# Order of the early loads in an attention and mixer kernel: q and k of pair 2 ahead of the sink rows

## The chip, the cores and the metric

The kernel runs on one core of a Trainium2 chip. A core has four compute engines that appear below by short names: TensorE (PE, with its weight loads as PEld), VectorE (DVE), ScalarE (ACT) and GpSimd (POOL). A fifth one, SyncE (SP), computes nothing and issues data transfers (DMAs); POOL issues some too. The transfers of both are carried out by the same 16 DMA engines. Every engine works through its own list of instructions in order and waits for others through semaphores.

The metric is the device time of one execution in microseconds (us). Less is better.

## The reference

The inputs are q, k and v (batch 4, 8 heads, 768 positions, head dimension 64) and four weight matrices. First comes attention in which each position sees a window of 128 positions up to itself and, beside it, the first 4 positions, the sinks:

```python
keep = is_sink | in_window            # pos < 4, or 0 <= query - key < 128
scores = np.where(keep, q @ k.T / sqrt(64), -1e9)
a = softmax(scores)
x = (a @ v) with the heads side by side    # (4, 768, 512)
```

Its result goes through a mixer of two stages with a residual each:

```python
h = np.maximum(x.T @ w_tok1, 0) @ w_tok2   # over the 768 positions, through 256
u = x + h.T
h2 = np.maximum(u @ w_ch1, 0) @ w_ch2      # over the 512 channels, through 1536
out = u + h2                               # (4, 768, 512) float32
```

## The kernel before

**Pairs.** Attention is done two heads at a time. There are 16 pairs, four for each batch; pair 0 to 3 are those of batch 0. For a pair, q and k are brought to bfloat16, turned on PE so that the head dimension lies on the partitions, multiplied, put through the exponential on ACT, masked, and multiplied with v. The two mixer stages of a batch follow and are interleaved with the attention of the next one.

**Early loads.** SP loads q and k of pairs 0 to 3 as float32 straight into the tile `early`: `load_raw` (L121) issues one DMA for q and one for k, 384 KB each. They are cast on the core, by ACT and DVE for pairs 0 to 2 and by POOL for pair 3 (`cast`, L1303; `copy`, L169). All other loads of inputs and weights are issued by POOL, which has them cast to bfloat16 on the way (`load_cast`, `load_v`, `load_w`).

**Sink rows.** The first four rows of v of each head are needed as a separate matrix, in which two pairs share a group of 32 partitions. The float32 tile `v_sink_f` (L238) is cleared by DVE; then four small DMAs on SP (L240 to L247, 2 KB each) put the sink rows of batch 0 into it, each followed by a DVE instruction that sets its column of ones. One POOL instruction (queued at L1310, run through `copy`, L173) casts it to `v_sink`. PE multiplies with `v_sink` in every half of every pair's last product (`pv`).

**What sets the order.** `in_order` keeps the instructions of an engine in the order in which the program issues them. The first part of the program is issued by hand: loads of pairs 0 and 1 (L186), a few matmuls on ones, masks and constants, the sink rows (L240), the loads of pairs 2 and 3 (L248), and v of pair 0 on POOL (L249). What follows is ordered by a planner (`Plan`) which simulates the engines with costs written into the program, takes whichever step could begin first and so fixes each engine's list. When the early loads land it doesn't work out: they stand as constants, for the casts at L1307 and for the sinks at L1310. On POOL its list begins with v of pair 0 and q of pair 4 and goes on with the cast of the sinks, v of pairs 1 and 2, `w_tok1`, v of pair 3, the cast of q of pair 3, `w_tok2`, the cast of k of pair 3, and more weights.

The lines of the planner that give the landing times:

```python
for p, at in enumerate(((3900.0, 5300.0), (7500.0, 8600.0), (11300.0, 12500.0), (13500.0, 14700.0))):
    for n, name in enumerate(("q_bf", "k_bf")):
        queue((name, p), cast(p, n, at[n]))
v_sink = Op({"POOL": 650.0}, lambda e: copy(e, v_sink0, v_sink_f), [landed(9000.0)])
```

Of the kernel before, what the change touches and what calls it, by code (L numbers as in the profile page):

```python
# [16 lines left out]
def kernel(  # L17
# [23 lines left out]
    NHP = H // 2  # L41
# [64 lines left out]
    def rows_of(pidx, n):  # L106

        b, hp = pairs[pidx]
        return (q, k)[n][b, 2 * hp:2 * hp + 2].rearrange(
            "h (j p) d -> p h j d" if pidx >= BY_DMA else "h (p j) d -> p h j d", j=NT,  # L110
        )
# [9 lines left out]
    def load_raw(pidx):  # L121
        raw = []
        for n in range(2):
            f = early[:, 2 * pidx + n]
            in_order(nc.sync.dma_start(out=f, in_=rows_of(pidx, n).rearrange("p h j d -> p h (j d)")))  # L125
            raw.append(f.rearrange("p h (j d) -> p h j d", j=NT))
        return raw
# [26 lines left out]
    def load_v(pidx):  # L154
        b, hp = pairs[pidx]
        v_aug = v_buf[pidx % NV]
        in_order(nc.gpsimd.dma_start(  # L157
            out=v_aug.rearrange("p i t d -> p (i t) d")[:, :, 0:D],
            in_=v[b].rearrange("h s d -> (h s) d")[2 * hp * S:2 * (hp + 1) * S].rearrange("(n p) d -> p n d", p=P),
        ))  # L160
        return v_aug
# [24 lines left out]
    raws = {p: load_raw(p) for p in range(2)}  # L186
# [50 lines left out]
    ODD = D // 2  # L237
    v_sink_f = singles.tile([P, NHP, 2, D1], FP32)  # L238
    in_order(nc.vector.memset(v_sink_f, 0.0))
    for n in range(4):  # L240
        i, odd = n // 2, n % 2
        rows = slice(D * i + ODD * odd, D * i + ODD * odd + n_sink)
        in_order(nc.sync.dma_start(
            out=v_sink_f[rows, odd::2, i, 0:D],
            in_=v[0].rearrange("(p o i) s d -> i o s p d", i=2, o=2)[i, odd, 0:n_sink],
        ))
        in_order(nc.vector.memset(v_sink_f[rows, odd::2, i, D:D1], 1.0))  # L247
    raws.update({p: load_raw(p) for p in range(2, NHP)})  # L248
    vs[0] = load_v(0)  # L249

    w_tok1 = singles.tile([P, NT, DTOK], BF16)
# [1141 lines left out]
```

## Time and profile before

| | |
|---|---|
| median of 3 runs | 196.14 us (195.31 to 196.88) |
| the profiled execution | 194.44 us |
| its span, first to last instruction | 192.7 us |
| PE busy in the span | 185.8 us |
| POOL busy in the span | 60.5 us, nearly all of it in the first half |
| granted clock of PE | 1.00 |

The profile is of one execution. Its times count from the start of the span. A row of the timeline gives the start, the time, the engine, the line of the kernel, the operation, what it writes and reads, and how many instructions are merged; in brackets stands how long the engine sat idle before it and what ended that. An engine named with a q (SPq, POOLq) is the part that issues DMAs. A row of the chain of work gives start, duration and what ran or was waited for. The time of a busy engine is not work alone: PE's instructions overlap, so a PE that is shown busy may still have small gaps between its instructions.

### The profile page before, as it was taken

To read this page: it belongs to the slowest core of one execution; us is meant where nothing else is said; L and a number is where in the kernel's file an instruction comes from. 1 tells how busy PE (TensorE), PEld (TensorE's weight loads), DVE (VectorE), ACT (ScalarE), POOL (GpSimd) and SP (SyncE) were. 2 spreads that over 40 slices of the span, in tenths; PEclk is the share of its full clock that TensorE was granted. 3 is DMA by queue.
4 is the path that set the end of the run, shared out by engine and by line. 5 is a ranking of instruction groups with operands and counts; after the bars stand their busy time and mean duration, and the time that the engine had idled before them with its cause. 6 is when DMAs were issued, how large, how long until landed. Compare 5 with 4: busy or idle time off the path is not lost.

```text
span 192.7 us, 5797 instructions
## 1 busy us (share of the span) xinstructions
PE 185.8 (96%) x2491; PEld 129.8 (67%) x2491; DVE 134.4 (70%) x299; ACT 106.3 (55%) x183; POOL 60.5 (31%) x78
## 2 busy tenths in 40 slices
PE   6898999999999999999999999999999999999993
PEld 1345995567764564666668888767678886567882
DVE  4768777898976647689778787847678771047672
ACT  4898767878865216879663433778642005764000
POOL 7299663765944951537810000000000000000000
PEclk9999999999999999999999999999999999999999
DMA  5999999999999999999999953400040435000016
GB/s 186 287 293 172 203 202 194 187 194 181 176 122 147 188 186 187 195 184 155 111 138 149 161 117 143 178 0 3 0 82 3 83 112 218 0 0 3 27 67 234
DMA packets 82138, 26.34 MB, mean 137 GB/s; under 512 B 69952, under 2 KB 79296, under 8 KB 82112
## 3 DMA queue, kind: packets, MB, share of 16 engines
q0 software_dynamic: 56864, 11.80, 74.8%
q1 hardware_dynamic: 25248, 14.17, 34.0%
q8 instruction: 19, 0.31, 0.7%
q14 instruction: 7, 0.06, 0.1%
HBM read 26.75 MB, written 6.29 MB: 171 GB/s over the span
## 4 chain that ended last, share of the span: by engine, by line
PE 88%; DMA 6%; DVE 1%; POOL 1%; SPq 0%; ACT 0%; issue 0%
PE ps_mx L164 77%; PE ps_sc L164 9%; DMA early<-in_q_dram 6%; PE ps_sc L496 1%; PE ps_mx L167 1%; PE ps_mx L496 1%; DVE kT L173 0%; SPq L125 0%; POOL k_bf L173 0%; POOL q_bf L173 0%; ACT qT L171 0%; POOL w_tok L182 0%; DVE o_sb L1100 0%; DVE v1T L179 0%; DVE ps_sc L545 0%
## 5 line engine op out<-in xcount | busy, mean ns | idle before, releaser
L164 PE MATMUL ps_mx<-uT,w_ch 128*128 128x384 bf16 x384 | 69.2, 326 | 0.0
L177 ACT ACTIVATE v1T<-ps_mx 128x384 bf16<-128x384 f32 x83 | 40.7, 490 | 36.1 <-PE ps_mx L164 35.5
L612 ACT ACTIVATE pT<-ps_sc 128x1024 bf16<-128x1024 f32 (+1 forms) x48 | 44.2, 954 | 19.6 <-PE ps_sc L164 19.4
L164 PEld LDWEIGHTS <-w_ch 128*128 128x128 bf16 x384 | 35.9, 98 | 21.3 <-issue 0.9
L164 PE MATMUL ps_mx<-w_ch,v1T 128*128 128x256 bf16 (+1 forms) x168 | 29.6, 318 | 0.0
L164 PEld LDWEIGHTS <-v1T 128*128 128x128 bf16 x234 | 22.5, 98 | 10.0 <-issue 0.5
L164 PEld LDWEIGHTS <-early 128*128 128x128 bf16 x222 | 21.3, 98 | 2.8
L164 PEld LDWEIGHTS <-w_tok 128*128 128x128 bf16 x240 | 19.5, 98 | 3.6 <-issue 0.2
L157 POOL DMA_DIRECT2D v_aug<-in_v_dram x16 | 16.7, 1050 | 7.5 <-PE ps_mx L164 5.1
L1255 DVE TENSOR_TENSOR early<-v1T 128x1152 bf16<-128x1152 bf16 x12 | 8.9, 754 | 13.8 <-ACT v1T L177 13.6
L829 DVE TENSOR_TENSOR u_sb<-ps_mx,x_sb 128x512 bf16<-128x512 f32 (+1 forms) x24 | 15.4, 654 | 2.9 <-PE ps_mx L164 2.6
L148 POOL DMA_DIRECT2D q_bf<-in_q_dram x16 | 13.2, 827 | 12.2 <-DMA q_bf<-in_q_dram 4.0
L164 PE MATMUL ps_mx<-w_sums,early 128*128 128x256 bf16 x126 | 15.9, 273 | 0.0
L164 PE MATMUL ps_mx<-v_aug,pT 128*128 128x65 bf16 x352 | 15.6, 193 | 0.0
L1100 DVE TENSOR_TENSOR o_sb<-ps_mx,u_sb 128x256 f32<-128x256 f32 x28 | 11.7, 422 | 5.3 <-PE ps_mx L164 5.1
L148 POOL DMA_DIRECT2D k_bf<-in_k_dram x16 | 13.3, 840 | 6.6 <-DMA v_aug<-in_v_dram 3.3
L164 PEld LDWEIGHTS <-pT 128*128 128x128 bf16 x352 | 13.8, 97 | 2.3 <-issue 0.4
L620 DVE TENSOR_TENSOR pT<-pT,mask_main 128x768 bf16<-128x768 bf16 (+1 forms) x25 | 14.6, 614 | 0.3 <-ACT pT L612 0.3
L164 PE MATMUL ps_sc<-qT,kT 64*32 64x160 bf16 (+3 forms) x480 | 14.2, 233 | 0.4 <-DVE ps_sc L545 0.2
L164 PE MATMUL ps_mx<-h1T,w_tok 128*128 128x256 bf16 (+1 forms) x120 | 14.2, 251 | 0.0
L164 PEld LDWEIGHTS <-kT 64*32 64x32 bf16 (+1 forms) x512 | 7.0, 91 | 9.1 <-issue 8.0
L164 PE MATMUL ps_mx<-x_sb,w_tok 128*128 128x256 bf16 (+1 forms) x120 | 12.2, 251 | 0.0
(84 smaller groups left out, 201.8 us busy)
## 6 DMA issues: line engine op xcount, KB each, us to landing
out_dram<-o_sb SPq DMA_DIRECT2D x22, 256.0 KB, 2.8
v_aug<-in_v_dram POOLq DMA_DIRECT2D x16, 192.0 KB, 9.4
w_ch<-in_moe_w_ch_dram POOLq DMA_DIRECT2D x8, 384.0 KB, 10.4
early<-in_q_dram SPq DMA_DIRECT2D x4, 384.0 KB, 5.2
early<-in_k_dram SPq DMA_DIRECT2D x4, 384.0 KB, 6.4
k_bf<-in_k_dram POOLq DMA_DIRECT2D x16, 96.0 KB, 11.3
q_bf<-in_q_dram POOLq DMA_DIRECT2D x16, 96.0 KB, 8.8
q_bf<-in_q_dram POOLq DMA_DIRECT2D x4, 192.0 KB, 9.4
```

The lines of the kernel that those rows point to most:

```text
L148: in_order(nc.gpsimd.dma_start(out=out[:, h], in_=rows[:, h]))
L157: in_order(nc.gpsimd.dma_start(out=v_aug.rearrange("p i t d -> p (i t) d")[:, :, 0:D], in_=v[b].rearrange("h s d -> (h s) d")[2 * hp * S:2 ...
L164: in_order(nc.tensor.matmul(*args, skip_group_check=True, **kwargs))
L167: in_order(nc.tensor.transpose(out, in_, ident))
L177: in_order(nc.scalar.activation(out, in_, AF.Relu))
L496: in_order(nc.tensor.transpose(outs[x][columns], block, ident[rows, rows]))
L612: in_order(nc.scalar.activation(part(tiles["pT", p][:, :, ds(2 * g, 2)]), of_keys(tiles["ps_s", p, g])[:, :, 0:width(g)], AF.Exp, scale=scale,
L620: in_order(nc.vector.tensor_tensor(out=pt, in0=pt, in1=m, op=ALU.mult))
L829: in_order(nc.vector.tensor_tensor(out=u_part(b, g, s0, n), in0=tiles["ps_u", b, g, s0], in1=x_sb[b][:, s0:s0 + n, c0:c0 + cn], op=ALU.add,))
L1100: in_order(nc.vector.tensor_tensor(out=o_sb, in0=ps, in1=u_rows(b, st)[:, g, cols] if first else o_sb, op=ALU.add,))
L1255: lambda e, n=n, x=x, y=y, how=how: in_order(nc.vector.tensor_tensor(out=v1_sums[:, n, ds(j, SUMMED)], in0=of(x), in1=of(y), op=how,)), deps,
```

## The change

The loads of q and k of pair 2, two DMAs on SP, are issued between the clearing of `v_sink_f` and the four small loads of the sink rows. Those of pair 3 stay behind the small loads. No instruction is added or taken away, no tile moves, and the planner's constants are the same.

```diff
     v_sink_f = singles.tile([P, NHP, 2, D1], FP32)
     in_order(nc.vector.memset(v_sink_f, 0.0))
+    raws[2] = load_raw(2)
     for n in range(4):
         i, odd = n // 2, n % 2
         rows = slice(D * i + ODD * odd, D * i + ODD * odd + n_sink)
...
         in_order(nc.vector.memset(v_sink_f[rows, odd::2, i, D:D1], 1.0))
-    raws.update({p: load_raw(p) for p in range(2, NHP)})
+    raws[3] = load_raw(3)
     vs[0] = load_v(0)
```

## The prediction

> **What bounds the kernel now.** I read the page's head first, then the chain of work that ended last.
>
> ```profile
> span 192.7 us, 5797 instructions
> PE 185.8 (96%) x2491; PEld 129.8 (67%) x2491; DVE 134.4 (70%) x299; ACT 106.3 (55%) x183; POOL 60.5 (31%) x78
> ```
>
> TensorE (PE) fills 96% of the span. So the question for any edit at the front is whether it delays PE's steady work. The chain of work shows what PE waits for there (start, duration, what):
>
> ```profile
> 1.76 5.26 DMA early<-in_q_dram
> ...
> 7.04 6.76 DMA early<-in_q_dram
> ...
> 13.86 0.82 POOL q_bf L173
> 14.68 0.65 POOL w_tok L182
> 15.33 0.84 POOL k_bf L173
> ...
> 16.22 0.35 PE ps_mx L505 x12
> ```
>
> The reader is to see a chain of loads (q of pair 1, whose landing at 7.02 us lets q of pair 3 be issued, which lands at 13.80), then a stretch on POOL, which casts q and k of pair 3 with a weight load's issue between them, and then PE. Busy time by stretches (bounds, length, then PE, PEld, DVE, ACT, POOL, PE clock, DMA share, GB/s) and PE's waits after 17 us say what a delay at this place is worth:
>
> ```profile
> 14.00:17.00 3.00, 1.92 (x69) 1.49 (x69) 2.07 (x4) 2.12 (x4) 3.00 (x5) 1.00 2.18 172
> ...
> 22.00:187.00 165.00, 164.81 (x2170) 117.84 (x2168) 117.47 (x250) 88.87 (x157) 44.30 (x52) 1.00 1.08 121
> ```
> ```profile
> PE ps_sc L164 <- DVE ps_sc L545: 0.2, 1, 0.2
> ```
>
> From 14 to 17 us PE is busy 1.92 of 3 us and POOL all of it. From 22 to 187 us PE is busy 164.81 of 165 us, and in the list of PE's waits from 17 to 188 us that one wait of 0.2 us is all there is. So almost nothing later can swallow a delay: what PE loses before 17 us, the end loses too, less about 0.2.
>
> **The change, part by part.** SP issues its twelve loads in this order (start, issue time):
>
> ```profile
> 2.26 0.47 SPq L125 DMA_DIRECT2D early<-in_k_dram  x1
> 2.81 1.36 SPq L243 DMA_DIRECT2D v_sink_f<-in_v_dram  x4
> 4.22 0.40 SPq L125 DMA_DIRECT2D early<-in_q_dram  x1
> 4.88 0.39 SPq L125 DMA_DIRECT2D early<-in_k_dram  x1
> 7.04 0.37 SPq L125 DMA_DIRECT2D early<-in_q_dram  x1
> 8.20 0.37 SPq L125 DMA_DIRECT2D early<-in_k_dram  x1
> ```
> ```profile
> SPq L125 <- DMA early<-in_q_dram: 1.8, 1, 1.8
> SPq L125 <- DMA early<-in_k_dram: 1.0, 2, 0.8
> ```
>
> These waits fit one rule: a load waits for the landing of the one eight places ahead of it. The tenth (k of pair 2, at 4.88) waits for the second, the eleventh (q of pair 3) for the third, the twelfth for the fourth. The change moves the fifth to eighth loads (sinks) behind the ninth and tenth. The eleventh and twelfth keep their places and the loads that they wait for, so the issues at 7.04 and 8.20 stay. Pair 2 is issued right behind 2.26 + 0.47, at about 2.75 and 3.25, some 1.5 us sooner. The sinks, 1.36 us of issuing, start at about 3.75; the last two of them become the ninth and tenth, and the last would be out at about 5.2, before the next load's 7.04. No instruction is added; nothing on SP ends later.
>
> What moves is the place in the queue. When do the data land? The engines that read them show it:
>
> ```profile
> 8.21 0.56 DVE L173 CAST k_bf<-early 128x768 bf16<-128x768 f32 x1 [0.60 <-DMA early<-in_k_dram]
> ...
> 11.69 0.57 DVE L173 CAST k_bf<-early 128x768 bf16<-128x768 f32 x1 [1.46 <-DMA early<-in_k_dram]
> ```
> ```profile
> 9.10 0.61 POOL L173 CAST v_sink<-v_sink_f 128x520 bf16<-128x520 f32 x1 [3.51 <-DMA v_sink_f<-in_v_dram]
> 9.66 2.21 POOL L157 DMA_DIRECT2D v_aug<-in_v_dram  x2
> 11.86 0.84 POOL L182 DMA_DIRECT2D w_tok<-in_moe_w_tok_dram  x1
> 12.67 1.04 POOL L157 DMA_DIRECT2D v_aug<-in_v_dram  x1
> ```
>
> k of pair 1 starts its cast at 8.21, the sinks theirs at 9.10, k of pair 2 at 11.69, each ending a wait for its load. The sinks were all issued by 4.17 (2.81 + 1.36), yet their 8 KB (32 rows of 64 floats) are read only 0.89 us behind k of pair 1, issued in front of them. I read this as a first-in, first-out queue: a small load waits for the large ones ahead. Put behind k of pair 2, the sinks should be ready at 11.69 + 0.89 = 12.58, **3.48 us later**. (That k of pair 2 lands sooner I cost at nothing: the stream ahead of it is the same but for 8 KB; the other end is the first rival.)
>
> The Trainium skill, page "DMA: Bandwidth & Descriptors", section "Queues, rings and completion order", states that each DMA engine takes a ring's descriptors in order, but that a load may use fewer than all 16 engines and completion between loads is then not in order. By this rule a sink could land ahead of the slowest share of k of pair 2, and the 0.89 would go at most: the loss would be 2.4 rather than 3.3. The trace agrees with the first half (9.10 behind 8.21); the second half no row of before decides.
>
> Now what stands behind. POOL runs in program order: behind the sinks' cast come two v loads, a weight load and a third v load, and then the cast of q of pair 3. From 9.10 to 12.67 + 1.04 = 13.71 POOL has no wait that the timeline marks; the next cast began at 13.86, when its load had landed. So there is 0.15 us of slack. A sinks' cast at 12.58 ends this block at 12.58 + 4.61 = 17.19, and q of pair 3 is cast at 17.19 rather than 13.86: **3.33 us late**, and then k of pair 3 by the same amount, as POOL is full through 17 us. What PE sees:
>
> ```profile
> 11.52 0.23 PE L164 MATMUL ps_mx<-v_sink,pT_sink 128*128 128x130 bf16 x1
> ...
> 13.44 0.60 PE L164 MATMUL ps_sc<-mask_add,ident 128*128 128x512 bf16 x2
> 14.74 0.35 PE L505 MATMUL ps_mx<-ident,q_bf 64*128 64x64 bf16 x12 [0.70 <-POOL q_bf L173]
> ```
>
> PE first meets the sinks at 11.52. Their cast would end at 12.58 + 0.61 = 13.19, so PE stands 1.7 us there; today's cast ends at 9.71 and has 1.8 us of cover. This isn't added to the other loss: PE's work from 11.52 to 14.04 moves to about 15.7, and the next step, at 14.74, needs the q that POOL casts, now 14.74 + 3.33 = 18.07. PE waits twice, and the second wait sets the sum. ACT and DVE follow PE there and get no later than it. POOL's loads are issued 3.4 us later too, but their readers on PE are also 3.3 late, and with POOL silent the queue's competition for pair 3 is less; I cost this at nothing (other end: a weight that lands later than it is needed, up to 0.5).
>
> Sum: **+3.3 us**, less at most 0.2 swallowed. The profiled execution took 194.44 us (192.7 of span and 1.74 around it) and would take 197.7; it lay 1.7 under the median of the runs. I carry the difference to the median 196.14: **199.4 us**.
>
> How far can the 3.3 be off? POOL's own loads share the engines with SP's queue. Packets of the two queues from 8 to 9 us, when the first POOL loads run, and from 11.3 to 12.3, where the sinks would be (packets, MB, share):
>
> ```profile
> q0 software_dynamic: 799, 0.10, 159.6%
> q1 hardware_dynamic: 94, 0.13, 35.6%
> ```
> ```profile
> q1 hardware_dynamic: 171, 0.26, 74.2%
> q0 software_dynamic: 95, 0.06, 40.6%
> ```
>
> Today the sinks pass before the first stretch. A sink load of four rows and two pairs is 8 packets, so 32 in all. If they sit on four engines, 8 on each, and an engine passes 171/16 = 11 packets of SP's queue in a microsecond, they add up to 0.7; at 94/16 = 6, up to 1.3. So the sum reaches from 2.4 (no lag behind k of pair 2) over 3.3 to 4.6. I take 3.3, as 0.89 is the only measured lag.
>
> **The rivals.**
>
> *Pair 2 is pulled forward.* Before, q of pair 2 waited to be issued. If SP's queue ran short of work for that, its earlier issue moves all behind it. The rates:
>
> ```profile
> 2.00:3.00 1.00, 1.00 (x4) 0.32 (x3) 0.87 (x9) 0.02 (x1) 0.98 (x2) 1.00 0.84 278
> 3.00:4.00 1.00, 1.00 (x4) 0.30 (x2) 0.12 (x2) 0.15 (x1) 0.94 (x3) 1.00 1.05 387
> 4.00:5.00 1.00, 0.85 (x12) 0.25 (x12) 0.11 (x1) 0.69 (x1) 1.00 (x2) 1.00 0.89 244
> ```
>
> For it: the rate falls from 387 to 244 GB/s. Against it: q and k of pair 1 had been issued by 2.73 and were not yet in, so the queue wasn't empty. If k of pair 2 lands 1.5 sooner, the sinks are ready at 11.1 and the loss is 1.8: **197.9**, a change within 1%.
>
> *Not slower.* The same mechanism in full: six loads of 128 rows by 768 floats are 2.36 MB; at 387 GB/s from 2 us on, where the data begin to flow, they'd be in at 8.1, the sinks 0.89 behind at 9.0. The point that decides is 9.25 (9.10 and the 0.15 of slack): sinks that are ready by then cost nothing, and PE could gain the 0.15 at most, as POOL's block then ends at 13.7. That, or sinks that don't queue behind the large loads, in which case the change does nothing to them, gives **196.0**. Against both: the sinks waited 4.9 us from 4.17 to 9.10, and from 8 us on POOL's packets take the engines.
>
> *The clock drops.* PE would stand from about 15.7 to 18.07. At the start it ran slow:
>
> ```profile
> 1.46 3.17 PE L164 MATMUL ps_mx<-ones 128*128 128x512 bf16 x7 [1.46 <-DVE ones L191]
> ...
> 4.78 0.51 PE L505 MATMUL ps_mx<-ident,q_bf 64*128 64x64 bf16 x12
> ...
> 7.69 0.34 PE L505 MATMUL ps_mx<-ident,q_bf 64*128 64x64 bf16 x12
> ```
>
> Twelve turns took 0.51 us at 4.78 and 0.34 later, so the slow pace lasted from 1.46 to about 5.3. Should the wait bring it back for as long, 3.8 x (1 - 0.34/0.51) = 1.3 us come on top: **200.7**. Against it: the granted clock stays at 1.00 through the stretch from 14 to 17 us, with over a third of it idle. The Trainium skill, page "TensorE: Matmul & The Clock Gate", section "Why this matters for your kernels", asks for no idle gaps over about 3 us; by that rule a gap of 2.4 us keeps the clock. No row of before has a gap so long.
>
> **How the numbers follow.** Forecast, sinks queue behind pair 2 and POOL hands the delay on: 0.74, at 199.4. Pulled forward, or half of the delay swallowed later: 0.12, at 197.9. Not slower: 0.04, at 196.0. Clock: 0.10, at 200.7. The range: the forecast's own 2.4 to 4.6 is 198.5 to 200.7; with the first rival below and the clock on the upper half, 197.4 to 201.3, which leaves out the last case and the tails. One per cent is 1.96 us, about what a measurement of this kernel can tell from no change. Slower by over 1%: 0.84 and part of the 0.12, 0.85; within: 0.12; faster: 0.03.
>
> **What would show it.** In the changed kernel's profile: SP issues q and k of pair 2 at about 2.75 and 3.25 and pair 3 still at 7.04 and 8.20; POOL's cast of v_sink starts near 12.6 behind a wait of some 7 us for its load; k of pair 2 is cast near 11.7 still; q of pair 3 near 17.2; PE shows a wait near 11.5 for v_sink and one of some 2 us near 18; from there all rows stand 3.3 later. I am wrong if v_sink is cast much before 11.7, if q of pair 3 isn't bound by POOL, or if PE closes the gap after 20 us.

## The result, and the profile after

The changed kernel is slower, by much less than forecast. Its median is 197.16 us (20 runs) against 195.58 us (20 runs of the kernel before). The ratio is 1.0074, with a 95% interval of 1.0045 to 1.0103: +1.45 us, where +3.3 was forecast. The three runs shown ahead of the prediction had a median of 196.14; with twenty it is 195.58. (The ratio leaves out the runs more than 1.5% above their kernel's fastest; there are more of those among the changed kernel's, and the section on PE's clock says why.) The profiled execution took 196.42 us. The first line of its page:

```profile
span 194.6 us, 5798 instructions
```

The span is 1.9 us longer than the profiled one of before. SP's issues, from the timeline:

```profile
2.77 0.47 SPq L125 DMA_DIRECT2D early<-in_q_dram  x1
3.28 0.47 SPq L125 DMA_DIRECT2D early<-in_k_dram  x1
3.80 2.29 SPq L244 DMA_DIRECT2D v_sink_f<-in_v_dram  x4
8.02 0.39 SPq L125 DMA_DIRECT2D early<-in_q_dram  x1
```

The order is as the change says, and pair 2 is issued at the forecast times. The sinks take 2.29 us to issue instead of 1.36. The rows that decide, from the timelines of POOL, DVE and PE:

```profile
11.29 0.64 POOL L173 CAST v_sink<-v_sink_f 128x520 bf16<-128x520 f32 x1 [5.89 <-DMA v_sink_f<-in_v_dram]
...
14.78 1.05 POOL L157 DMA_DIRECT2D v_aug<-in_v_dram  x1
15.79 0.88 POOL L173 CAST q_bf<-early 128x768 bf16<-128x768 f32 x1
```
```profile
11.37 0.97 DVE L173 CAST k_bf<-early 128x768 bf16<-128x768 f32 x1
```
```profile
12.96 0.23 PE L164 MATMUL ps_mx<-v_sink,pT_sink 128*128 128x130 bf16 x1
...
16.72 0.35 PE L506 MATMUL ps_mx<-ident,q_bf 64*128 64x64 bf16 x12 [1.38 <-POOL q_bf L173]
```

POOL waits 5.89 us for the sinks (3.51 before) and casts them 2.19 us later than before, at 11.29. Its block behind takes 4.50 us without a gap, so q of pair 3 is cast at 15.79 instead of 13.86, 1.93 later, and PE turns it at 16.72 instead of 14.74, 1.98 later. PE has no wait at its first product with the sinks: it comes there only at 12.96, and the cast ended at 11.93. The long stretch behind, in the columns of the prediction's rows:

```profile
22.00:187.00 165.00, 164.81 (x2186) 117.75 (x2184) 118.25 (x250) 90.57 (x160) 45.49 (x54) 1.00 1.05 122
```

From 22 us on PE is as full as before, so the 1.98 us stay to the end.

### The profile page after: what moved, and what is told of

It is laid out like the page before. It is cut to its first block, busy times and chain, and to the rows that moved or that the text cites. A ratio compares the mean times of both kernels' runs of the same rounds, so it can differ in the third digit from the quotient of the medians.

```text
span 194.6 us, 5798 instructions
## 1 busy us (share of the span) xinstructions
PE 187.0 (96%) x2491; PEld 130.2 (67%) x2491; DVE 135.7 (70%) x299; ACT 106.5 (55%) x183; POOL 60.2 (31%) x78
## 4 chain that ended last, share of the span: by engine, by line
PE 87%; POOL 4%; DMA 3%; SPq 2%; DVE 1%; issue 0%; ACT 0%; POOLq 0%
PE ps_mx L164 76%; PE ps_sc L164 9%; DMA v_sink_f<-in_v_dram 3%; POOL v_aug L157 2%; SPq L125 1%; SPq L244 1%; PE ps_sc L497 1%; POOL w_tok L182 1%; PE ps_mx L167 1%; PE ps_mx L497 1%; DVE kT L173 0%; POOL k_bf L173 0%; POOL q_bf L173 0%; ACT qT L171 0%; POOL v_sink L173 0%
## 5 line engine op out<-in xcount | busy, mean ns | idle before, releaser
L164 PE MATMUL ps_sc<-qT,kT 64*32 64x160 bf16 (+3 forms) x480 | 14.7, 235 | 0.2 <-DVE ps_sc L546 0.2
## 6 DMA issues: line engine op xcount, KB each, us to landing
k_bf<-in_k_dram POOLq DMA_DIRECT2D x16, 96.0 KB, 11.2
```

The lines of the kernel that those rows point to most:

```text
L164: in_order(nc.tensor.matmul(*args, skip_group_check=True, **kwargs))
```

## The experiments

Theory P is that POOL's block, held by the sinks, hands its lateness to PE through the casts of pair 3. What was open was why the loss is 1.45 and not 3.3. The expectations name others beside it. Theory E: the loss comes from the loads of pair 1, which land later, and from a PE that reaches its full pace later. Theory N: the first profile of before lay low. Theory C: PE's clock makes part of the loss. Rival D: POOL's late loads cost time by themselves.

**The two kernels again.** Two more executions of each were profiled, with no edit.

> The kernel before once more, to see how much of its own early part differs between executions: is the first one typical, with q of pair 1 cast at 7.04, PE at full clock from 5.62, q of pair 3 cast at 13.86 and a span of 192.7? Theory N (the execution before that was profiled lay low, and a usual one is bound a little later by its loads): q of pair 1 is cast near 7.9 in a usual execution too, q of pair 3 at 14.4 to 15, and the span is near 194.2. Theory P in its plain form: q of pair 3 is cast at 13.9 again, as POOL and its loads are the same.

> The kernel before, a third execution with a profile. Theory N (the first one lay low): q of pair 3 is cast at 14.3 to 15.0 again, not at 13.86, and the span is 193.3 to 194.3. If the first one was typical: 13.9 and 192.7.

> The changed kernel once more. Theory P (POOL's block): the cast of v_sink starts at 11.0 to 11.6, q of pair 3 is cast 4.5 us behind it, and the span ends 1.7 to 2.2 us later than the kernel before. Theory E (early loads): the loss comes from q and k of pair 1, which land about 1 us later once q and k of pair 2 are issued right behind them, and from a PE that gets its full clock later (9.67 instead of 5.62 us); then the cast of q of pair 1 at 8.0 instead of 7.04 comes again, and the loss goes up and down with it from one execution to the next.

> The changed kernel, a third execution with a profile. Theories P and N together: the cast of v_sink at 11.2 to 11.9, q of pair 3 at 15.7 to 16.3, and the last instruction 178.7 to 179.3 us behind that cast, if the granted clock is full throughout; 1.2 to 1.7 us later where it falls to half for 3.4 us behind the gap on PE.

The kernel before, second and third execution: POOL's casts, and DVE's cast of k of pair 2.

```profile
9.84 0.61 POOL L173 CAST v_sink<-v_sink_f 128x520 bf16<-128x520 f32 x1 [4.44 <-DVE k_bf L173]
...
14.96 0.82 POOL L173 CAST q_bf<-early 128x768 bf16<-128x768 f32 x1 [0.57 <-DMA early<-in_q_dram]
```
```profile
13.18 0.58 DVE L173 CAST k_bf<-early 128x768 bf16<-128x768 f32 x1 [1.25 <-DMA early<-in_k_dram]
```
```profile
9.34 0.61 POOL L173 CAST v_sink<-v_sink_f 128x520 bf16<-128x520 f32 x1 [3.94 <-DMA v_sink_f<-in_v_dram]
...
13.98 0.82 POOL L173 CAST q_bf<-early 128x768 bf16<-128x768 f32 x1
```
```profile
12.76 0.56 DVE L173 CAST k_bf<-early 128x768 bf16<-128x768 f32 x1 [2.29 <-DMA early<-in_k_dram]
```

The changed kernel, second and third:

```profile
11.57 0.80 POOL L173 CAST v_sink<-v_sink_f 128x520 bf16<-128x520 f32 x1 [6.17 <-DVE q_bf L173]
...
16.17 0.88 POOL L173 CAST q_bf<-early 128x768 bf16<-128x768 f32 x1
```
```profile
12.05 0.80 POOL L173 CAST v_sink<-v_sink_f 128x520 bf16<-128x520 f32 x1 [6.66 <-DVE q_bf L173]
...
16.66 0.86 POOL L173 CAST q_bf<-early 128x768 bf16<-128x768 f32 x1
```

The kernel before isn't the same in its early part from one execution to the next: its spans are 192.7, 194.0 and 193.1 us. In the second, POOL stood 0.57 us waiting for q of pair 3 itself, so there the sinks had 0.57 of slack, not 0.15. The expectation that this is the usual case fell: in the third, the cast is at 13.98. The spans of the changed kernel are 194.6, 195.1 and 195.9. On the mean of three the sinks' cast moves from 9.43 to 11.64 (+2.2), the cast of q of pair 3 from 14.27 to 16.21 (+1.9), and the span from 193.3 to 195.2 (+1.9). The timed runs, more of them, say +1.45, with an interval of 0.9 to 2.0. Timed again, the changed kernel has a ratio of 1.0075 (1.0042 to 1.0108). The kernel before, timed against itself, has 1.0023 (0.9994 to 1.0052), so the small ratios further down, 1.003 to 1.005, are close to what no change gives.

The first half of theory E falls: the cast of q of pair 1 late, at 8.03, which the changed kernel showed at first, belongs to no order of the loads. The load of q of pair 3 waits on SP for q of pair 1; it is issued at 8.18 in the kernel before, second execution, and at 7.44 in the changed one, third:

```profile
8.18 0.37 SPq L125 DMA_DIRECT2D early<-in_q_dram  x1
```
```profile
7.44 0.39 SPq L125 DMA_DIRECT2D early<-in_q_dram  x1
```

Its second half came in all three executions of the changed kernel: PE reaches its full pace later. Twelve turns there still take 0.51 to 0.53 us at about 9.15, where the kernel before needs 0.34 or 0.35 for the same step (at 7.69, 8.80 and 8.02). That is one reason why PE comes to the sinks at 12.96 and not at 11.52. But the kernel with seven copies below has it too, with all loads in their old order (0.50 at 8.82), and the table below shows that it isn't in the loss.

**When k of pair 2 lands.** The list of DMA issues in a narrow window gives one load's time from issue to landing (the last number). First the kernel before, three executions (issued at 4.88, 5.74 and 4.99), then the changed one, three (issued at 3.28, 3.28 and 3.29):

```profile
early<-in_k_dram SPq DMA_DIRECT2D x1, 384.0 KB, 6.8
```
```profile
early<-in_k_dram SPq DMA_DIRECT2D x1, 384.0 KB, 7.4
```
```profile
early<-in_k_dram SPq DMA_DIRECT2D x1, 384.0 KB, 7.7
```
```profile
early<-in_k_dram SPq DMA_DIRECT2D x1, 384.0 KB, 8.0
```
```profile
early<-in_k_dram SPq DMA_DIRECT2D x1, 384.0 KB, 8.0
```
```profile
early<-in_k_dram SPq DMA_DIRECT2D x1, 384.0 KB, 7.8
```

It lands at 11.7, 13.1 and 12.7 before and at 11.3, 11.3 and 11.1 after the change: 1.3 us sooner on the mean. And the sinks don't follow it by a steady 0.89. In the chains of work of the changed kernel's three executions their last load lands at 5.63 + 5.44 = 11.07, at 11.36 and at 11.84, so 0.2 us ahead of k of pair 2, then 0.1 and 0.7 behind:

```profile
5.63 5.44 DMA v_sink_f<-in_v_dram
```
```profile
6.42 4.94 DMA v_sink_f<-in_v_dram
```
```profile
5.66 6.18 DMA v_sink_f<-in_v_dram
```

Why k of pair 2 lands sooner stays open, but two reasons can be left out. POOL's silence isn't it: with seven and nine copies on POOL (next) and the old order of loads, POOL's later loads start only at 11.30 and 13.70, and k of pair 2 still lands at 12.3 and 12.6. Nor is it that SP's queue had run short of work: q of pair 2, issued 1.5 us sooner, lands no sooner (10.0, 10.0 and 10.2; in two executions of the kernel before 9.4 and 9.6), and from 4 to 5 us the transfers run at 206, 204 and 280 GB/s in the changed kernel and at 244, 255 and 237 in the kernel before.

**POOL late, all loads in their old order.** Nine copies on POOL go ahead of the cast; in a second kernel, seven.

```diff
+    def late_cast(e):
+        for _ in range(9):
+            copy("POOL", w_sums[:, 0, 0:2].rearrange("p f c -> p (f c)"), ones)
+        copy(e, v_sink0, v_sink_f)
+
-    v_sink = Op({"POOL": 650.0}, lambda e: copy(e, v_sink0, v_sink_f), [landed(9000.0)])
+    v_sink = Op({"POOL": 650.0}, late_cast, [landed(9000.0)])
```

> The kernel before, all loads in their old order, with nine copies of 128x512 on POOL ahead of the cast of v_sink, so that POOL alone is late. Theory P: the end moves by as much as that cast starts after 9.25 us, less 0.2 at most: +1.9 if it starts at 11.3. Theory E: pair 1 lands as before (cast of its q at 7.04), so there is no loss, under 0.3 us.

> As the kernel with nine copies on POOL ahead of the cast of v_sink, but with seven: the cast starts at about 11.2, where the changed kernel has it, with all loads in their old order. Theory P: the same loss as the changed kernel, 0.5 to 1.0%. If the order of the loads matters beside POOL's lateness, the two differ by more than 0.5 us in executions at full clock.

Seven copies, POOL and then PE:

```profile
10.74 0.62 POOL L173 CAST v_sink<-v_sink_f 128x520 bf16<-128x520 f32 x1
...
15.41 0.85 POOL L173 CAST q_bf<-early 128x768 bf16<-128x768 f32 x1
```
```profile
16.32 0.35 PE L505 MATMUL ps_mx<-ident,q_bf 64*128 64x64 bf16 x12 [1.11 <-POOL q_bf L173]
```

The sinks' cast came at 10.74 rather than at 11.2, so the dose was smaller than planned: the cast of q of pair 3 is 1.1 us behind the mean of before, and the ratio is 1.0035 (1.0004 to 1.0067), +0.7 us. The expected 0.5 to 1.0% was for the larger dose; against the changed kernel, q of pair 3 is cast 0.8 us sooner and the median is 0.9 lower, which leaves little for the order of the loads. Nine copies put the casts at 12.81 and 17.56 (table below); the ratio is 1.0196 (1.0156 to 1.0236), +3.8 us, of which a part is PE's clock (further down). POOL late by itself, with the loads untouched, makes the loss, and the more of it the later.

**More and fewer loads ahead of the sinks.** The first kernel, shown against the one before, has q of pair 2 alone ahead (`load_one` issues one of the two DMAs of `load_raw`). The second, against the changed one, has pair 3 ahead too.

```diff
     in_order(nc.vector.memset(v_sink_f, 0.0))
+    raws[2] = [load_one(2, 0)]
...
-    raws.update({p: load_raw(p) for p in range(2, NHP)})
+    raws[2].append(load_one(2, 1))
+    raws[3] = load_raw(3)
```
```diff
     raws[2] = load_raw(2)
+    raws[3] = load_raw(3)
...
-    raws[3] = load_raw(3)
```

> Only q of pair 2 is issued ahead of the four sink loads, k of pair 2 stays behind them. Theory P: the sinks land right behind q of pair 2, their cast starts at 9.3 to 10.2, so the end moves by 0.1 to 1.0 us. Theory E: pair 1 is followed by a large load as in the changed kernel, its q lands about 1 us late, and most of the loss is there: 1 us or more.

> q and k of pair 3 too are issued ahead of the sink loads. Theory P: the sinks land behind k of pair 3, so their cast starts at 14.3 to 15.5, q of pair 3 is cast 4.5 us later, at 19 to 20, and executions at full clock end 4 to 5.5 us later than those of the kernel before; the gap of some 4 us on PE costs the clock in nearly every execution, for 1 to 2 us more. If POOL's block is not what binds, the loss stays at the changed kernel's.

q of pair 2 alone, POOL and then DVE:

```profile
10.13 0.91 POOL L178 CAST v_sink<-v_sink_f 128x520 bf16<-128x520 f32 x1 [4.73 <-DVE kT L178]
...
14.84 0.86 POOL L178 CAST q_bf<-early 128x768 bf16<-128x768 f32 x1
```
```profile
12.83 0.60 DVE L178 CAST k_bf<-early 128x768 bf16<-128x768 f32 x1 [2.27 <-DMA early<-in_k_dram]
```

The sinks land behind q of pair 2, within the range expected; k of pair 2, behind them again, is cast at 12.83, as in the kernel before. The ratio is 1.0040 (1.0004 to 1.0075), +0.8 us. With pair 3 ahead too:

```profile
14.57 0.61 POOL L173 CAST v_sink<-v_sink_f 128x520 bf16<-128x520 f32 x1 [9.06 <-DMA v_sink_f<-in_v_dram]
...
18.99 0.87 POOL L173 CAST q_bf<-early 128x768 bf16<-128x768 f32 x1
```

The sinks' cast is where it was expected and that of q of pair 3 at the lower edge, and the ratio is 1.0274 (1.0233 to 1.0315), +5.4 us, here too with a part from PE's clock.

**The law of the delay.** Each profiled execution in which POOL casts pair 3 gives one line, but for the kernel with the sinks first, where PE waits for something else: the cast of the sinks, the cast of q of pair 3, and the span. The line with six matmuls and the last two are taken up below it.

| kernel | sinks cast | q of pair 3 cast | span | span less that cast |
|---|---|---|---|---|
| before | 9.10 | 13.86 | 192.7 | 178.8 |
| before, third | 9.34 | 13.98 | 193.1 | 179.1 |
| before, second | 9.84 | 14.96 | 194.0 | 179.0 |
| q of pair 2 alone ahead | 10.13 | 14.84 | 194.0 | 179.2 |
| seven copies on POOL | 10.74 | 15.41 | 194.2 | 178.8 |
| changed | 11.29 | 15.79 | 194.6 | 178.8 |
| changed, second | 11.57 | 16.17 | 195.1 | 178.9 |
| changed, with six matmuls on PE | 11.90 | 16.31 | 195.6 | 179.3 |
| changed, third | 12.05 | 16.66 | 195.9 | 179.2 |
| nine copies on POOL | 12.81 | 17.56 | 197.8 | 180.2 |
| pair 3 ahead too | 14.57 | 18.99 | 200.7 | 181.7 |

Over 2.8 us of lateness the rest of the kernel is 179.0 us long within 0.3: nothing later swallows any of it. That is theory P, one to one. The last two lines lie 1.2 and 2.7 above it.

**PE's clock.** Those two have what the others haven't, in the column before the DMA share (the granted clock). First nine copies, then PE's gap and two stretches with pair 3 ahead:

```profile
18.00:20.00 2.00, 1.14 (x46) 0.81 (x48) 0.86 (x2) 1.13 (x2) 2.00 (x4) 1.00 1.36 127
20.00:23.40 3.40, 3.40 (x47) 2.33 (x48) 3.04 (x8) 2.87 (x5) 3.40 (x5) 0.50 1.69 175
```
```profile
19.91 0.35 PE L506 MATMUL ps_mx<-ident,q_bf 64*128 64x64 bf16 x12 [2.30 <-POOL q_bf L173]
```
```profile
20.00:23.00 3.00, 2.74 (x70) 2.15 (x70) 2.03 (x4) 2.70 (x4) 3.00 (x5) 0.55 1.48 151
23.00:27.00 4.00, 4.00 (x38) 1.80 (x37) 2.47 (x7) 1.76 (x3) 3.40 (x5) 0.50 1.41 179
```

Behind a wait of PE for q of pair 3, 2.32 us in the first and 2.30 in the second, the clock is granted at half, for 3.4 us in the first and for about twice that in the second. The length of a wait alone doesn't decide it: with pair 3 ahead PE had waited longer before, for the sinks, and kept the full clock up to 20 us:

```profile
15.24 0.22 PE L164 MATMUL ps_mx<-v_sink,pT_sink 128*128 128x130 bf16 x1 [3.15 <-POOL v_sink L173]
```

This falls on some executions of the changed kernel too: the mean granted clock of an execution lay below 0.995 in 11 of its 32 timed runs (9 of 20 and 2 of 12), and in 7 of 88 of the kernel before. It lay there in 5 of 6 runs with nine copies and in all 6 with pair 3 ahead, but also in 6 of 12 with q of pair 2 alone ahead and in 3 of 12 with seven copies, whose profiles show no wait of PE over 1.1 us behind its start. In the twenty, the median of those below was 198.70 us and of the others 196.80. To test it, six matmuls went into the gap:

```diff
+            if (p, n) == (3, 0):
+                keep_warm(6, given["mx"][0])
             ps = [bank("mx", NT, D, dtype=BF16) for _ in range(2)]
```

> The changed kernel with six matmuls of ones (128x512, about 1.3 us in all) on PE ahead of the turn of q of pair 3, in the gap in which PE waits for POOL. Theory C (part of the loss is PE's clock, which falls to half for 3.4 us after the gap in a share of the executions): mean granted clocks of 0.983 to 0.991, which 11 of 32 executions of the changed kernel showed, become rare (1 in 10 or fewer), the median falls by 0.3 to 0.8 us, and executions at full clock stay at 196.8 to 197.1. Theory P alone: nothing changes, or the six matmuls cost up to 0.3 us.

```profile
15.18 1.46 PE L164 MATMUL ps_mx<-ones 128*128 128x512 bf16 x6
17.24 0.35 PE L506 MATMUL ps_mx<-ident,q_bf 64*128 64x64 bf16 x12 [0.60 <-POOL q_bf L173]
```

None of 8 timed runs was below 0.995, as expected; since the second set of runs without the matmuls had only 2 of 12, that can be chance. The median didn't fall: 197.20 us, ratio 1.0082 (1.0054 to 1.0110). The halved clock is an extra in some executions; it isn't what the median's 0.74% is made of.

**Pair 3 freed from POOL.** The casts of pair 3 are carried out by DVE, in the kernel before and in the changed one.

```diff
-        return Op(cost, lambda e: copy(e, bf_tile(p, n), raws[p][n]), [landed(at)])
+        return Op(cost, lambda e: copy("DVE" if p == NHP - 1 else e, bf_tile(p, n), raws[p][n]), [landed(at)])
```

> The changed kernel with q and k of pair 3 cast by DVE instead of POOL, in the same place of the program, so that they no longer stand behind POOL's late block; the sinks and POOL's other loads are as late as before that. Theory P: the cast of q of pair 3 starts with its landing, 14.3 to 14.9, PE turns it at 15.0 to 15.5 (16.7 to 17.2 in the changed kernel), and the time falls by 1 to 1.6 us, to that of the kernel before or a little under it. Rival D (the late loads of v and weights cost time by themselves): over half of the loss stays, the kernel is 0.7 us or more slower than before, and PE shows a new wait for a load between 17 and 30 us.

> The kernel before with the same move of the two casts to DVE. Theory P: POOL's block hardly held them in the old order, so this gains little, 0 to 0.5 us against the kernel before, and it lies within 0.4 us of the changed kernel with that move. Rival D: it is 0.7 us or more faster than the changed kernel with that move.

The changed loads with that move, POOL and PE, then the old loads with it:

```profile
11.16 0.61 POOL L173 CAST v_sink<-v_sink_f 128x520 bf16<-128x520 f32 x1 [5.76 <-DMA v_sink_f<-in_v_dram]
```
```profile
15.78 0.35 PE L506 MATMUL ps_mx<-ident,q_bf 64*128 64x64 bf16 x12
...
17.65 0.33 PE L506 MATMUL ps_mx<-ident,k_bf 64*128 64x64 bf16 x11 [0.26 <-DVE qT L173]
```
```profile
8.61 0.61 POOL L173 CAST v_sink<-v_sink_f 128x520 bf16<-128x520 f32 x1 [3.22 <-DMA v_sink_f<-in_v_dram]
```
```profile
15.50 0.35 PE L505 MATMUL ps_mx<-ident,q_bf 64*128 64x64 bf16 x12 [0.52 <-DVE x_sb L683]
...
17.58 0.33 PE L505 MATMUL ps_mx<-ident,k_bf 64*128 64x64 bf16 x11 [0.26 <-DVE qT L173]
```

POOL is 2.55 us later in the one than in the other, its loads of v and weights with it, and the spans are 194.8 and 194.8. PE shows no wait for a load between 17 and 30 us in either. So the late loads cost nothing by themselves here, and the casts of pair 3 are the way by which POOL's lateness reaches PE. They aren't far from costing something: in the third execution of the changed kernel, where POOL was latest, PE waited 0.16 us at 22.77 for `w_tok`, which POOL had issued at 14.84. In time the two have ratios of 1.0049 (1.0018 to 1.0080) and 1.0028 (0.9994 to 1.0062) to the kernel before, 0.4 us apart, with intervals that overlap; they leave room for a small cost of the late loads that the spans don't show. The changed loads with the move are still over 0.7 us slower than the kernel before, which was a sign of rival D; the old loads with the move, where POOL is early, show where that comes from. The expectation that the move wins back the loss fell: k of pair 3 now stands in DVE's list and is turned at 17.6, where POOL's cast in the kernel before allowed 16.22 to 17.32. What the move saves on q it loses on k.

**Sinks first.** The four small loads, with the clearing of their tile, go between pair 0 and pair 1: the block from L237 to L247 moves to where the second mark of omission stands.

```diff
-    raws = {p: load_raw(p) for p in range(2)}
+    raws = {0: load_raw(0)}
...
     keep_warm(7, 0)
...
+    raws[1] = load_raw(1)
```

> The four sink loads are issued between pair 0 and pair 1, and the clearing of v_sink_f stands ahead of the mask's. The cast of v_sink then no longer waits, and POOL goes on at about 5.6 instead of 9.1 us. Theory P in its plain form: nothing is lost, and as q of pair 3 is bound by its landing at 13.80 the end stays within 0.3 us. Rival: POOL's wait had held back its own loads, which now run against q and k of pairs 2 and 3; those land 1 us or more later and the end moves by +0.5 to +2 us.

```profile
4.61 1.14 POOL L157 DMA_DIRECT2D v_aug<-in_v_dram  x1
...
6.44 0.75 POOL L173 CAST v_sink<-v_sink_f 128x520 bf16<-128x520 f32 x1
...
12.76 0.82 POOL L173 CAST q_bf<-early 128x768 bf16<-128x768 f32 x1 [1.56 <-DMA early<-in_q_dram]
```
```profile
14.36 0.28 PE L164 MATMUL ps_mx<-v_aug,pT 128*128 128x65 bf16 x4 [1.66 <-DMA v_aug<-in_v_dram]
```

Neither side had this. POOL is free early and q of pair 3 is cast 1.1 us sooner than in the profile of before, but PE waits 1.66 us for v of pair 0: the clearing of the sinks' tile pushed the mask's back on DVE, so POOL issued that load at 4.61 instead of 3.55. It also took 9.7 us from issue to landing, where it took 8.1 in the profile of before. Behind that gap the clock is at half again:

```profile
14.70:18.10 3.40, 3.40 (x42) 1.64 (x38) 2.04 (x5) 1.19 (x2) 3.33 (x5) 0.50 2.02 176
```

The ratio is 1.0045 (1.0011 to 1.0078). It says that the block ahead of the sinks' cast matters too; it doesn't test theory P, and a version of it that keeps v of pair 0 early wasn't tried. No version beat the kernel before.

## Why the forecast had the right sign and the wrong size

- *What bounds the kernel*: right. Delay before 17 us comes out at the end one to one (the table).
- *SP's issues*: right for pair 2 (2.77 and 3.28). Pair 3 didn't keep 7.04 and 8.20, but those move from execution to execution in the kernel before as well. The last sink load was out at 6.09 rather than 5.2, still ahead of pair 3.
- **The failed step: "the sinks should be ready at 11.69 + 0.89 = 12.58, 3.48 us later".** Measured: 11.29, 11.57 and 12.05, on the mean 2.2 later. Both terms were mis-sized. "That k of pair 2 lands sooner I cost at nothing" was wrong: it lands at 11.2 instead of 12.5 on the mean of three (11.7 in the execution that the forecast used, an early one). And the lag of 0.89 isn't a constant: from the landing of k of pair 2 to the cast of the sinks it was 0.0, 0.3 and 1.0. Of the 1.3 us between 3.48 and 2.2, k of pair 2 makes 0.5 (11.2 against 11.69), the lag 0.5 (0.4 on the mean) and the base 0.3 (the sinks' cast in the kernel before is at 9.43 on the mean, not at 9.10). The Trainium skill, page "DMA: Bandwidth & Descriptors", section "Queues, rings and completion order", had said that completion between loads isn't in order when one of them uses fewer engines. The trace agrees in one execution of three, with 11.07 against 11.3; in the other two the sinks land behind. How many engines the sinks used no run here shows. That the lag could go was in the forecast, as the low end of its range; what wasn't is a k of pair 2 that lands sooner by itself, so the +1.9 of the profiles lies below that end.
- *The range*: its upper end, 4.6, adds up to 1.3 for the sinks' own packets to a sum that already holds the lag of 0.89. Counted from 2.4, the sum without a lag, they give 3.7.
- *POOL's block*: right. 4.61 us was forecast, 4.42 to 5.12 was measured from one cast to the other, and its lateness went to q of pair 3.
- *The slack of 0.15*: from one execution. It was 0.57 in another, and that takes a further part of the loss from the time of a usual run. The three profiles' mean (+1.9) lies above the timed runs' +1.45 but inside their interval of 0.9 to 2.0; three executions of each, which differ by 1.3 us among themselves, can't tell the two apart.
- *PE waits twice*: only once. In the changed kernel PE came to the sinks at 12.96, with their cast done at 11.93. The wait for q of pair 3 was 1.38, 1.76 and 1.49 us instead of some 2.
- *Loads costed at nothing*: right within its own bound. The 0.16 us for `w_tok` in one execution is all that PE lost to a load that POOL issued late, and up to 0.5 was allowed.
- *Rivals*: "pair 2 is pulled forward", with the sinks ready at 11.1 and a loss of 1.8, has the numbers that came; it had 0.12. Its reason isn't borne out: the rate falls between 4 and 5 us after the change too, and q of pair 2 lands no sooner. That its numbers fit is luck as far as is known. "Not slower" didn't happen: the sinks do queue behind large loads. "The clock drops" is real, in about a third of the changed kernel's executions; 1.3 us was forecast for it and 1.9 lie between the medians. The Trainium skill's rule there (page "TensorE: Matmul & The Clock Gate", section "Why this matters for your kernels", no gaps over about 3 us) doesn't hold as a threshold here: 2.3 us were enough in two kernels, and 3.15 us in one of them left the clock at 1.00.

## What to carry to other kernels

A small load behind large ones in the same queue is about as late as they are (here from 0.2 us ahead to 0.7 behind), and an engine that waits for it in program order passes the delay to all that stands behind it; look there for something that the critical engine needs. Before a term of a forecast is taken from one profiled execution, ask what in it would be different in the next one: a slack of 0.15 us or a lag of 0.89 us that was measured once is not a price. And when a load is issued sooner, don't cost its earlier landing at nothing: what lands behind it moves too.

## What the runs showed of the hardware

- Two executions of the same kernel, without any edit, differ by 1.1 us in when k of pair 2 is cast (11.69 and 12.76) or by 1.5 (13.18), and by 1.3 us in their span.
- PE's clock fell to half for 3.4 us behind waits of 2.32 and of 1.66 us, and for about twice that behind one of 2.30. Waits of 3.15 and of 1.76 us left it at 1.00. The changed kernel's wait of 1.4 to 1.8 us may be what costs the clock in a share of its executions; where in those it fell wasn't seen, as none of them was profiled.
- Issuing the same four small loads took SP 1.36 to 1.53 us behind four large loads and 2.29 to 2.92 us behind six, in three executions each.
- SP's loads wait for the landing of the load eight places ahead also where the small ones come last: with pair 3 ahead too, the last sink load, the twelfth, is issued at 8.72, when k of pair 1, the fourth, has landed (2.26 + 6.44 = 8.70).
